# Transposing two weight matrices by DMA from DRAM instead of on TensorE, with the input loads on three queues

## The chip, the cores and the metric

The kernel runs on one core of one Trainium2 chip. The metric is device time in microseconds (us); lower is better. The engines are named as in the profile: PE (TensorE, matrix products; PEld is its weight load), DVE (VectorE), ACT (ScalarE), POOL (GpSimd), SP (SyncE). Every run quoted here as a time was marked fast (a run over 1.5% above the fastest of its kernel would be marked slow). Single profiled probes of one core are used for durations inside the trace, not for times. Each kernel was profiled once.

## The reference, cut to what matters

Two layers, each a linear attention followed by a gated MLP, over one sequence of 2048 rows and width 512, all in bf16:

```python
qkv = (x_norm @ wqkv).reshape(B, S, 3, H, Dh)            # H = 32 heads of Dh = 16
pk  = einsum("bhsd,hdf->bhsf", k, w_phi)                 # per head: k @ w_phi ; pq likewise
phi = concat([softmax(pk), softmax(-pk)])                # and the same for pq
kv, z = sum over s of phi_k^T v, sum over s of phi_k     # then num / den with phi_q, then @ wo
x = x + attention(layernorm(x));  x = x + mlp(layernorm(x))      # twice
```

The kernel multiplies `w_phi` into the weights once: `Wk2 = Wk @ Wblk` and `Wq2 = Wq @ Wblk`, where `Wblk` holds `w_phi` as diagonal blocks. This is called folding. The kernel writes that product as `matmul(..., lhsT=wT, rhs=Wblk)`, with Wk as `wT`: Wk with its *output* dimension on the partitions, that is, transposed. The whole change is about how that transposed copy is made, and when.

## The kernel before

Loads: SP's queue brings X, ScalarE's queue brings the weights. Wk and Wq come as they are.

```python
nc.gpsimd.dma_start(out=wf[:], in_=...w_phi...)
nc.sync.dma_start(out=st.X[0][:, 0:2, :], in_=xv[:, 0:2, :])
nc.scalar.dma_start(out=wk[:], in_=wv[:, :, D:2 * D])
nc.sync.dma_start(out=st.X[0][:, 2:4, :], in_=xv[:, 2:4, :])
nc.scalar.dma_start(out=wv_t[:], in_=wv[:, :, 2 * D:3 * D])
for c in range(1, st.NC):
    nc.sync.dma_start(out=st.X[c][:], in_=xv[:, c * TPC:(c + 1) * TPC, :])
nc.scalar.dma_start(out=wq[:], in_=wv[:, :, 0:D])
nc.scalar.dma_start(out=wo[:], in_=...)
```

Folding transposes on PE, copies on ACT, multiplies on PE, and copies on DVE:

```python
def fold(name, w):
    dst = const.tile([P, NDB, D], BF16, name=name)
    wT = st.big.tile([P, NDB, D], BF16, name="wT", tag="hT")
    for m in range(NDB):                                   # NDB = 4
        tps = st.ps_a.tile([P, NDB, P], BF16, name="tps", tag="a")
        for b in range(NDB):
            nc.tensor.transpose(out=tps[:, b, :], in_=w[:, m, b * P:(b + 1) * P], identity=ident[:])
        nc.scalar.copy(out=wT[:, :, m * P:(m + 1) * P], in_=tps[:])
    for m in range(NDB):
        wps = ...                                          # 4 matmuls wT x Wblk
        nc.vector.tensor_copy(out=dst[:, m, :]..., in_=wps[:])
    return dst
st.Wk2 = fold("Wk2", wk)
st.fold_q = lambda: fold("Wq2", wq)
```

Each tile of 128 rows is normalised on ACT (`xn`, from the row statistics and `nm`, the negated mean times the reciprocal deviation) and transposed by a DMA on SP's queue (`xnTA`). The key stage then makes per tile `kps` (keys), `vps` (values) and `kvq` (the sum over rows); `R` is built at its end. Wq is folded in one block before tile 10:

```python
def ahead(t):
    if t % 2 == 0 and t + 4 < st.T:
        with tc.issue_after(first.ins):
            A.norm(t + 4, 2)                # statistics, nm, xn and xnTA of two later tiles
    if 2 <= t < 9:
        st.load_B(A.moved)                  # two of the MLP's weight loads on SP's queue
    if t == 10:
        st.Wq2 = st.fold_q()
weave(A.keys(0, st.T, lag=2, pin=True, each=ahead), 1.0, none, 1.0)
```

The softmax here doesn't subtract the row's maximum and nothing guards it: scores larger than these inputs give would overflow.

## Time and profile before

| | before |
|---|---|
| median of 3 runs | 450.06 us (449.75 to 451.85) |
| span of the profiled execution | 446.8 us |
| first key matmul (`kps`) starts | 16.22 us |
| tile 9 / tile 10 of the keys start | 39.99 / 48.67 us |
| `R` starts, end of the key stage | 66.8 us |

These are lines of the page of the kernel before. In part 1, an engine's busy time is followed by its share and its instructions. In part 2 each position is a fortieth of the span (11.2 us). In part 6 the last number is the median time from issue to landing.

```profile
span 446.8 us, 7042 instructions
...
PE 394.1 (88%) x2508; PEld 226.2 (51%) x2508; DVE 276.4 (62%) x604; ACT 287.5 (64%) x653; POOL 70.1 (16%) x88
...
DMA  8659400211111121132001000011211132120010
GB/s 247 177 129 296 99 0 13 42 31 35 38 25 35 37 59 37 27 79 48 1 16 33 1 13 12 12 37 35 54 43 47 38 70 49 34 60 25 13 36 23
...
X<-in_A_x_dram SPq DMA_DIRECT2D x3, 512.0 KB, 11.5
```

PE is the limit over the whole span. Only the first slices are different: there the DMA engines are busy and PE waits. The table by stretch (start:end, length, busy time of each engine with its instructions, then granted clock, DMA share, GB/s) shows how full the DMA engines are at the start:

```profile
4.00:6.00 2.00, 0.03 (x1) 0.03 (x2) 1.21 (x3) 0.00 (x0) 0.00 (x0) 1.00 1.08 382
...
8.00:10.00 2.00, 0.59 (x6) 0.59 (x6) 1.38 (x9) 1.65 (x6) 0.00 (x0) 1.00 1.11 350
...
12.00:14.00 2.00, 0.41 (x4) 0.31 (x3) 2.00 (x5) 0.93 (x2) 0.00 (x0) 1.00 1.09 385
14.00:16.00 2.00, 0.17 (x2) 0.00 (x0) 2.00 (x7) 0.00 (x0) 0.00 (x0) 1.00 1.19 327
```

The chain of waits that ends last goes through the start like this (start, duration, what):

```profile
1.32 5.41 DMA X<-in_A_x_dram
...
8.79 0.58 ACT wT L109
...
10.58 5.59 DMA xnTA<-xn
...
16.22 1.04 PE kps L199 x2
```

The second loss is seen in the timeline of PE around the fold of Wq (start, duration, engine, line, operation; in brackets the idle time before it, and what ended that):

```profile
39.99 1.03 PE L199 MATMUL kps<-Wk,xnTA 128*128 128x512 bf16 x4
...
45.48 0.38 PE L108 MATMUL tps<-ident,wq 128*128 128x128 bf16 x4 [0.76 <-ACT wT L109]
...
48.44 0.40 PE L113 MATMUL wps<-Wblk,wT 128*128 128x128 bf16 x4 [1.49 <-ACT wT L109]
48.67 1.03 PE L199 MATMUL kps<-Wk,xnTA 128*128 128x512 bf16 x4
```

From tile 9 to tile 10 there are 8.7 us, where later tiles take 2.2. This is what the change aims at.

### The profile page before, as it was taken

How to read it: one execution, taken by the hardware profiler on the slowest of the kernel's cores; microseconds unless marked ns; L12 is line 12 of the kernel's file. 1: busy time of each engine (PE TensorE's matmuls, PEld its weight loads, DVE VectorE, ACT ScalarE, POOL GpSimd, SP SyncE). 2: the span in 40 equal slices, each digit the busy share in tenths (PEclk: the TensorE clock that was granted, in tenths of full speed). 3: DMA queues.
4: the chain of work that ended last, by engine and by line, in shares of the span. 5: the costliest groups of instructions: out<-in, count | busy, mean ns of one | idle time of the engine just before them, and what ended most of it. 6: DMA issues, size and time to landing. Idle time of an engine off the chain costs nothing.

```text
span 446.8 us, 7042 instructions
## 1 busy us (share of the span) xinstructions
PE 394.1 (88%) x2508; PEld 226.2 (51%) x2508; DVE 276.4 (62%) x604; ACT 287.5 (64%) x653; POOL 70.1 (16%) x88
## 2 busy tenths in 40 slices
PE   2688788899988999979998998778998899999996
PEld 2244444367756444435445744336675644444474
DVE  4795767737677777647465755773676676742232
ACT  4598756995846476599645749686584646736442
POOL 1077480000000000014323431000000000000000
PEclk9999999999999999999999999998999999999999
DMA  8659400211111121132001000011211132120010
GB/s 247 177 129 296 99 0 13 42 31 35 38 25 35 37 59 37 27 79 48 1 16 33 1 13 12 12 37 35 54 43 47 38 70 49 34 60 25 13 36 23
DMA packets 61458, 23.57 MB, mean 53 GB/s; under 512 B 52864, under 2 KB 60400, under 8 KB 61424
## 3 DMA queue, kind: packets, MB, share of 16 engines
q1 hardware_dynamic: 59280, 21.02, 20.6%
q10 hardware_dynamic: 2112, 2.10, 1.5%
q8 instruction: 19, 0.31, 0.3%
q14 instruction: 15, 0.12, 0.1%
q0 software_dynamic: 32, 0.02, 0.0%
HBM read 8.44 MB, written 2.10 MB: 24 GB/s over the span
## 4 chain that ended last, share of the span: by engine, by line
PE 57%; ACT 18%; DMA 9%; DVE 6%; issue 6%; POOL 2%; SPq 0%; POOLq 0%; ACTq 0%; DVEq 0%
PE ybps L394 13%; PE gps L377 12%; PE ups L384 12%; ACT xn L156 5%; PE yaps L314 4%; PE kps L199 4%; PE qps L268 4%; PE vps L209 4%; DMA oT<-o 3%; DMA xnTA<-xn 3%; PE kvq L238 2%; ACT junk L360 2%; ACT ru L387 2%; DMA xnTB<-xn 2%; ACT Eq L270 1%
## 5 line engine op out<-in xcount | busy, mean ns | idle before, releaser
L377 PE MATMUL gps<-xnTB,wg 128*128 128x256 bf16 (+3 forms) x528 | 99.7, 310 | 4.1 <-DMA xnTB<-xn 2.1
L384 PE MATMUL ups<-xnTB,wu 128*128 128x256 bf16 (+3 forms) x528 | 99.2, 310 | 3.3 <-ACT rg L380 3.3
L388 DVE TENSOR_TENSOR hT<-rg,ru 128x256 bf16<-128x256 bf16 (+3 forms) x132 | 48.7, 370 | 64.3 <-ACT ru L387 63.8
L394 PE MATMUL ybps<-wd,hT 128*128 128x512 bf16 (+1 forms) x352 | 80.8, 379 | 2.7 <-ACT ru L387 2.0
L380 ACT ACTIVATE rg<-gps 128x256 bf16<-128x256 f32 (+3 forms) x132 | 60.0, 454 | 34.2 <-PE gps L377 31.8
L221 POOL TENSOR_TENSOR phiK<-ek,sk 128x1024 bf16<-128x1024 bf16 x30 | 57.8, 1929 | 88.2 <-DVE sk L218 38.6
L387 ACT CAST ru<-ups 128x256 bf16<-128x256 f32 (+3 forms) x132 | 58.1, 440 | 18.1 <-PE ups L384 13.8
L377 PEld LDWEIGHTS <-wg 128*128 128x128 bf16 (+1 forms) x528 | 52.3, 101 | 32.8 <-DMA xnTB<-xn 3.4
L384 PEld LDWEIGHTS <-wu 128*128 128x128 bf16 (+1 forms) x528 | 52.6, 101 | 29.3 <-issue 4.3
L216 DVE TENSOR_REDUCE sk<-ek 128x64 f32<-128x1024 bf16 x32 | 38.9, 1217 | 31.1 <-ACT ek L205 30.9
L394 PEld LDWEIGHTS <-hT 128*128 128x128 bf16 (+1 forms) x352 | 34.3, 98 | 43.9 <-issue 2.8
L156 ACT ACTIVATE xn<-X,nm,rstd 128x512 bf16<-128x512 bf16 x64 | 49.7, 813 | 9.1 <-DMA xnTA<-xn 5.5
L360 ACT ACTIVATE junk<-X,mean 128x512 bf16<-128x512 bf16 x32 | 23.1, 721 | 36.8 <-POOL mean L357 36.5
L292 DVE TENSOR_TENSOR Tn<-erq,rS 128x816 bf16<-128x816 f32 x64 | 45.9, 717 | 1.0
L397 DVE TENSOR_TENSOR X<-X,ybps 128x512 bf16<-128x512 bf16 x32 | 21.9, 685 | 30.8 <-PE ybps L394 30.5
L357 POOL TENSOR_SCALAR mean<-xsum 128x1 f32<-128x1 f32 x32 | 7.1, 223 | 208.8 <-DVE X L320 104.8
L199 PE MATMUL kps<-Wk,xnTA 128*128 128x512 bf16 x128 | 34.2, 389 | 5.2 <-DMA xnTA<-xn 4.8
L268 PE MATMUL qps<-xnTA,Wq 128*128 128x512 bf16 x128 | 32.5, 378 | 6.8 <-ACT Eq L271 6.2
L314 PE MATMUL yaps<-wo,oT 128*128 128x512 bf16 x128 | 33.7, 379 | 4.0 <-DMA oT<-o 4.0
L209 PE MATMUL vps<-wv,xnTA 128*128 128x512 bf16 x128 | 33.9, 387 | 0.0
L291 DVE RECIPROCAL rS<-erq 128x48 f32<-128x48 f32 x64 | 22.4, 350 | 15.5 <-PE erq L282 15.5
L204 ACT ACTIVATE ek<-kps 128x512 bf16<-128x512 f32 x32 | 19.1, 596 | 13.9 <-PE kps L199 13.9
(58 smaller groups left out, 388.7 us busy)
## 6 DMA issues: line engine op xcount, KB each, us to landing
out_dram<-X SPq DMA_DIRECT2D x16, 128.0 KB, 1.7
X<-in_A_x_dram SPq DMA_DIRECT2D x3, 512.0 KB, 11.5
wg<-in_B_W_gate_dram SPq DMA_DIRECT2D x4, 344.0 KB, 4.7
wu<-in_B_W_up_dram SPq DMA_DIRECT2D x4, 344.0 KB, 5.8
wd<-in_B_W_down_dram SPq DMA_DIRECT2D x5, 256.0 KB, 4.4
wk<-in_A_wqkv_dram ACTq DMA_DIRECT2D x1, 512.0 KB, 5.1
X<-in_A_x_dram SPq DMA_DIRECT2D x2, 256.0 KB, 4.7
wv<-in_A_wqkv_dram ACTq DMA_DIRECT2D x1, 512.0 KB, 8.0
```

The lines of the kernel that those rows point to most:

```text
L156: nc.scalar.activation(out=xn[:], in_=st.X[c][:, t0 + i, :], func=AF.Identity, scale=rstd[:, i:i + 1], bias=nm[:, i:i + 1])
L199: mm = nc.tensor.matmul(kps[:], lhsT=xnT[:, b, ts], rhs=st.Wk2[:, b, :], start=(b == 0), stop=(b == NDB - 1))
L209: mm = nc.tensor.matmul(vps[:], lhsT=xnT[:, b, ts], rhs=st.wv[:, b, :], start=(b == 0), stop=(b == NDB - 1))
L221: eng.tensor_tensor(out=phiK[:].rearrange("p s (h f) -> p (s h) f", f=DH), in0=ek[:].rearrange("p s (h f) -> p (s h) f", f=DH), in1=sk[:]. ...
L268: nc.tensor.matmul(qps[:], lhsT=st.Wq2[:, m, b * P:(b + 1) * P], rhs=self.xnT[c][:, m, :], start=(m == 0), stop=(m == NDB - 1))
L314: nc.tensor.matmul(yps[:], lhsT=oT[:, b, :], rhs=st.wo[:, b, :], start=(b == 0 and not on_pe), stop=(b == NDB - 1))
L377: nc.tensor.matmul(gps[:n, 0:w], lhsT=st.wg[:, b, f * P:f * P + n], rhs=xnT[:, b, 0:w], start=(b == 0), stop=(b == NDB - 1))
L380: nc.scalar.activation(out=rg[:n, 0:w], in_=gps[:n, 0:w], func=AF.Relu)
L384: nc.tensor.matmul(ups[:n, 0:w], lhsT=st.wu[:, b, f * P:f * P + n], rhs=xnT[:, b, 0:w], start=(b == 0), stop=(b == NDB - 1))
L387: nc.scalar.copy(out=ru[:n, 0:w], in_=ups[:n, 0:w])
L388: nc.vector.tensor_tensor(out=hT[:n, f, 0:w], in0=rg[:n, 0:w], in1=ru[:n, 0:w], op=Alu.mult)
L394: nc.tensor.matmul(yps[:], lhsT=hT[:n, f, (t - lo) * P:(t - lo + 1) * P], rhs=st.wd[:n, f, :], start=(f == 0), stop=(f == NFT - 1))
```

## The change

The intent: let the DMA engines transpose Wk and Wq on their way from DRAM (I call each such transfer of 128 rows, 128 KB, a *flip*), so that PE's 32 transposes and ACT's 8 copies go away; spread the input loads over three queues so that they are issued sooner; and spread the fold of Wq over tiles 6 to 9 so that no tile waits for all of it. Line numbers in the profiles are those of each kernel's own file.

```diff
+    def flip(dst, off):
+        for m in range(NDB):
+            st.moved = nc.sync.dma_start_transpose(out=dst[:, :, m * P:(m + 1) * P],
+                                                   in_=A_wqkv[m * P:(m + 1) * P, off:off + D])
     nc.gpsimd.dma_start(out=wf[:], ...)
-    nc.sync.dma_start(out=st.X[0][:, 0:2, :], in_=xv[:, 0:2, :])
-    nc.scalar.dma_start(out=wk[:], in_=wv[:, :, D:2 * D])
-    nc.sync.dma_start(out=st.X[0][:, 2:4, :], in_=xv[:, 2:4, :])
+    nc.scalar.dma_start(out=st.X[0][:, 0:2, :], in_=xv[:, 0:2, :])
+    flip(wkT, D)
+    nc.scalar.dma_start(out=st.X[0][:, 2:4, :], in_=xv[:, 2:4, :])
     nc.scalar.dma_start(out=wv_t[:], in_=wv[:, :, 2 * D:3 * D])
-    for c in range(1, st.NC):
-        nc.sync.dma_start(out=st.X[c][:], ...)
-    nc.scalar.dma_start(out=wq[:], in_=wv[:, :, 0:D])
-    nc.scalar.dma_start(out=wo[:], ...)
+    nc.scalar.dma_start(out=st.X[1][:], in_=xv[:, TPC:2 * TPC, :])
+    st.flip_q = lambda: flip(wqT, 0)
 ...  (masks for Wblk on GpSimd)
+    for c in range(2, st.NC):
+        nc.gpsimd.dma_start(out=st.X[c][:], ...)
+    nc.gpsimd.dma_start(out=wo[:], ...)
 ...
-    def fold(name, w):  (transposes on PE, copies on ACT, four products)
+    def fold(dst, wT, m):  (one of the four products; copy on DVE for even m, on ACT for odd m)
+    for m in range(NDB):
+        fold(st.Wk2, wkT, m)
+    st.fold_q = lambda m: fold(st.Wq2, wqT, m)
 ...
+        if t == 0:
+            st.flip_q()
-        if 2 <= t < 9:
+        if 3 <= t < 10:
             st.load_B(A.moved)
-        if t == 10:
-            st.Wq2 = st.fold_q()
+    def also(t):
+        if 6 <= t < 10:
+            st.fold_q(t - 6)
```

The diff also adds an `on_pool` branch to the normalisation, which is never taken, and cuts the query stage into one function per block (not shown; the order of its instructions stays).

More of the change, by code (lines that the diff above doesn't have):

```diff
@@ L56, in setup @@
     st.X = [const.tile([P, TPC, D], BF16, name=f"X{c}") for c in range(st.NC)]
-    wk = st.big.tile([P, NDB, D], BF16, name="wk", tag="Eq", bufs=4)
+    wkT = st.big.tile([P, NDB, D], BF16, name="wkT", tag="Eq", bufs=4)
+    wqT = st.big.tile([P, NDB, D], BF16, name="wqT", tag="Eq", bufs=4)
     wv_t = const.tile([P, NDB, D], BF16, name="wv")
-    wq = st.big.tile([P, NDB, D], BF16, name="wq", tag="Eq", bufs=4)
     wf = const.tile([P, NDB, DH], BF16, name="wf")
     wo = const.tile([P, NDB, D], BF16, name="wo")
+    def flip(dst, off):
+        for m in range(NDB):
+            st.moved = nc.sync.dma_start_transpose(out=dst[:, :, m * P:(m + 1) * P],
+                                                   in_=A_wqkv[m * P:(m + 1) * P, off:off + D])
     nc.gpsimd.dma_start(out=wf[:], in_=A_w_phi.rearrange("(b j) d f -> (j d) b f", b=NDB, j=8))
-    nc.sync.dma_start(out=st.X[0][:, 0:2, :], in_=xv[:, 0:2, :])
-    nc.scalar.dma_start(out=wk[:], in_=wv[:, :, D:2 * D])
-    nc.sync.dma_start(out=st.X[0][:, 2:4, :], in_=xv[:, 2:4, :])
+    nc.scalar.dma_start(out=st.X[0][:, 0:2, :], in_=xv[:, 0:2, :])
+    flip(wkT, D)
+    nc.scalar.dma_start(out=st.X[0][:, 2:4, :], in_=xv[:, 2:4, :])
     nc.scalar.dma_start(out=wv_t[:], in_=wv[:, :, 2 * D:3 * D])
     nc.scalar.preload_act_table_set("natural_log_exp_and_others")
-    for c in range(1, st.NC):
-        nc.sync.dma_start(out=st.X[c][:], in_=xv[:, c * TPC:(c + 1) * TPC, :])
-    nc.scalar.dma_start(out=wq[:], in_=wv[:, :, 0:D])
-    nc.scalar.dma_start(out=wo[:], in_=A_wo.rearrange("(b p) f -> p b f", p=P))
+    nc.scalar.dma_start(out=st.X[1][:], in_=xv[:, TPC:2 * TPC, :])
     st.wv, st.wo = wv_t, wo
+    st.flip_q = lambda: flip(wqT, 0)
     st.eps = const.tile([P, 1], F32, name="eps")
@@ L85, in setup @@
     st.M8f = M8f
+    for c in range(2, st.NC):
+        nc.gpsimd.dma_start(out=st.X[c][:], in_=xv[:, c * TPC:(c + 1) * TPC, :])
+    nc.gpsimd.dma_start(out=wo[:], in_=A_wo.rearrange("(b p) f -> p b f", p=P))
     M8 = const.tile([P, 8], BF16, name="M8")
@@ L100, in setup, with fold @@
         st.vext.append(v)
-    def fold(name, w):
-        dst = const.tile([P, NDB, D], BF16, name=name)
-        wT = st.big.tile([P, NDB, D], BF16, name="wT", tag="hT")
-        for m in range(NDB):
-            tps = st.ps_a.tile([P, NDB, P], BF16, name="tps", tag="a")
-            for b in range(NDB):
-                nc.tensor.transpose(out=tps[:, b, :], in_=w[:, m, b * P:(b + 1) * P], identity=ident[:])
-            nc.scalar.copy(out=wT[:, :, m * P:(m + 1) * P], in_=tps[:])
-        for m in range(NDB):
-            wps = st.ps_b.tile([P, NDB, P], F32, name="wps", tag="b")
-            for b in range(NDB):
-                nc.tensor.matmul(wps[:, b, :], lhsT=wT[:, b, m * P:(m + 1) * P], rhs=Wblk[:, b, :],
-                                 start=True, stop=True)
-            nc.vector.tensor_copy(out=dst[:, m, :].rearrange("p (b f) -> p b f", f=P), in_=wps[:])
-        return dst
-    st.Wk2 = fold("Wk2", wk)
-    st.fold_q = lambda: fold("Wq2", wq)
+    st.Wk2 = const.tile([P, NDB, D], BF16, name="Wk2")
+    st.Wq2 = const.tile([P, NDB, D], BF16, name="Wq2")
+    def fold(dst, wT, m):
+        wps = st.ps_b.tile([P, NDB, P], F32, name="wps", tag="b")
+        for b in range(NDB):
+            nc.tensor.matmul(wps[:, b, :], lhsT=wT[:, b, m * P:(m + 1) * P], rhs=Wblk[:, b, :],
+                             start=True, stop=True)
+        out_ = dst[:, m, :].rearrange("p (b f) -> p b f", f=P)
+        if m % 2:
+            nc.scalar.copy(out=out_, in_=wps[:])
+        else:
+            nc.vector.tensor_copy(out=out_, in_=wps[:])
+    for m in range(NDB):
+        fold(st.Wk2, wkT, m)
+    st.fold_q = lambda m: fold(st.Wq2, wqT, m)
     st.wg = const.tile([P, NDB, F], BF16, name="wg")
@@ L137, in setup, with apply_norm @@
     return st
-def apply_norm(st, c, t0, n, var, scale, mean, sign, dst, col):
+def apply_norm(st, c, t0, n, var, scale, mean, sign, dst, col, on_pool=False):
     nc = st.nc
@@ L155, in apply_norm, with norm_tiles @@
         xn = st.work.tile([P, D], BF16, name="xn")
-        nc.scalar.activation(out=xn[:], in_=st.X[c][:, t0 + i, :], func=AF.Identity,
-                             scale=rstd[:, i:i + 1], bias=nm[:, i:i + 1])
+        if on_pool:
+            nc.gpsimd.tensor_scalar(out=xn[:], in0=st.X[c][:, t0 + i, :], scalar1=rstd[:, i:i + 1],
+                                    scalar2=nm[:, i:i + 1], op0=Alu.mult, op1=Alu.add)
+        else:
+            nc.scalar.activation(out=xn[:], in_=st.X[c][:, t0 + i, :], func=AF.Identity,
+                                 scale=rstd[:, i:i + 1], bias=nm[:, i:i + 1])
         moved = nc.sync.dma_start_transpose(out=dst[:, :, (col + i) * P:(col + i + 1) * P], in_=xn[:])
     return last, moved
-def norm_tiles(st, c, t0, n, dst, col):
+def norm_tiles(st, c, t0, n, dst, col, on_pool=False):
     nc = st.nc
@@ L168, in norm_tiles @@
         nc.vector.bn_aggr(out=mv[:, i, :], in_=stats[:])
-    return apply_norm(st, c, t0, n, mv[:, 0:n, 1], 1.0, mv[:, 0:n, 0], -1, dst, col)
+    return apply_norm(st, c, t0, n, mv[:, 0:n, 1], 1.0, mv[:, 0:n, 0], -1, dst, col, on_pool)
 class LayerA:
@@ L178, in __init__, with norm, keys @@
         self.moved = None
-    def norm(self, t, n=1):
+    def norm(self, t, n=1, on_pool=False):
         c, ti = t // TPC, t % TPC
-        last, self.moved = norm_tiles(self.st, c, ti, n, self.xnT[c], ti)
+        last, self.moved = norm_tiles(self.st, c, ti, n, self.xnT[c], ti, on_pool)
         return last
-    def keys(self, lo, hi, on_dve=(), lag=1, pin=False, each=None):
+    def keys(self, lo, hi, on_dve=(), lag=1, pin=False, each=None, also=None):
         st, nc = self.st, self.st.nc
@@ L229, in keys @@
                 yield 2.3
+            if also is not None:
+                also(t)
         for k in late:
@@ L260, in build_R, with query, queries @@
                                            op0=Alu.add, op1=Alu.mult)
-    def queries(self, c):
+    def query(self, c, b, keep=lambda ins: ins):
         st, nc = self.st, self.st.nc
-        self.Eq[c] = Eq = st.big.tile([P, NDB, 2, CH], BF16, name="Eq", bufs=st.NC)
-        for b in range(NDB):
-            qps = st.ps_a.tile([P, CH], F32, name="qps", tag="a")
-            for m in range(NDB):
-                nc.tensor.matmul(qps[:], lhsT=st.Wq2[:, m, b * P:(b + 1) * P], rhs=self.xnT[c][:, m, :],
-                                 start=(m == 0), stop=(m == NDB - 1))
-            nc.scalar.activation(out=Eq[:, b, 0, :], in_=qps[:], func=AF.Exp, scale=1.0)
-            nc.scalar.activation(out=Eq[:, b, 1, :], in_=qps[:], func=AF.Exp, scale=-1.0)
+        if b == 0:
+            self.Eq[c] = st.big.tile([P, NDB, 2, CH], BF16, name="Eq", bufs=st.NC)
+        Eq = self.Eq[c]
+        qps = st.ps_a.tile([P, CH], F32, name="qps", tag="a")
+        for m in range(NDB):
+            mm = nc.tensor.matmul(qps[:], lhsT=st.Wq2[:, m, b * P:(b + 1) * P], rhs=self.xnT[c][:, m, :],
+                                  start=(m == 0), stop=(m == NDB - 1))
+            if m == 0:
+                keep(mm)
+        nc.scalar.activation(out=Eq[:, b, 0, :], in_=qps[:], func=AF.Exp, scale=1.0)
+        nc.scalar.activation(out=Eq[:, b, 1, :], in_=qps[:], func=AF.Exp, scale=-1.0)
+    def queries(self, c, lo=0):
+        for b in range(lo, NDB):
+            self.query(c, b)
             yield 4
@@ L453, in ahead @@
                 A.norm(t + 4, 2)
-        if 2 <= t < 9:
+        if t == 0:
+            st.flip_q()
+        if 3 <= t < 10:
             st.load_B(A.moved)
-        if t == 10:
-            st.Wq2 = st.fold_q()
-    weave(A.keys(0, st.T, lag=2, pin=True, each=ahead), 1.0, none, 1.0)
-    weave(A.queries(0), QC, none, 1.0)
+    def also(t):
+        if 6 <= t < 10:
+            st.fold_q(t - 6)
+    weave(A.keys(0, st.T, lag=2, pin=True, each=ahead, also=also), 1.0, none, 1.0)
+    weave(A.queries(0), 1.0, none, 1.0)
     qs = seq(*[A.queries(c) for c in range(1, NC)]), 3 * QC
```

## The prediction

> **What bounds the kernel now.** Over the whole span TensorE is the limit (part 1 of the page: PE 394.1 of 446.8 us, 88%). The change touches only what lies before 67 us, where PE is not full: windows give PE busy 3.9 of the first 16.0 us, 23.5 of 16–42, 3.3 of 42–49, 13.0 of 49–62. After that the instruction order of both kernels is the same, so the key stage's gain should pass through one to one.
>
> Two losses are in reach:
> 1. The start. DMA moves about 350 GB/s from 4 to 16 us. The first row transpose (xnTA) issues at 10.58 and lands at 16.2, behind the X loads on its own ring; the first key matmul (kps) starts at 16.22.
> 2. Folding Wq in one block. kps of tile 9 starts at 39.99, of tile 10 at 48.67: 8.7 us against 2.20 in tiles 10–15. PE waits for the wT copies (0.59 us each on ACT, queued behind normalisations), not for xnTA, which were there. About 6.5 us lost.
>
> **Removed.** 32 PE transposes (3 us), 8 ACT copies (4.7 us).
>
> **Added.** 8 transposes from DRAM on SP's queue. SP issues an SBUF transpose in 1.19 us, so 8 take about 9.6 us and the first xnTA can issue at about 10.5 us: as before. In DMA time a transpose costs about 0.64 us (two in 16–20 us, share 0.32), against 0.36 us for 128 KB at 350 GB/s: some 2 us more DMA. [...]I expect no more bandwidth in the first 16 us (two queues reach 350 GB/s here). xnTA 0 now stands behind the flips rather than the X loads: landing at 13–16.5 us.
>
> **Moved.** In the new order VectorE builds Wblk only after statistics and nm of the second X block (before: ahead of them, done at 9.1 us). That nm waits for rstd on ScalarE, which stands behind the fourth xn, which needs a buffer freed by xnTA 0. So: X1 about 12 us, xnTA 0 about 13–16.5, nm 15–17.5, Wblk 16–18.5, 16 fold matmuls, two bnst (1.3 us) ahead of two copies of Wk2 on VectorE (0.69 each); on ScalarE two copies behind two xn. First kps at 18.5–22.5 us, say 20.3: about 4 us LATER than before.
> Against it: eight xn instead of four are done before the first kps. ScalarE from there through tile 9 needs about 24 us (1.48 per tile, 0.78 per xn, small ones, two Wq copies), PE 22.8 (1.73 + 0.47 per tile, 4 x 0.43 fold). So tile 10 starts 24.5–25.5 us after the first kps (before 32.4), at about 45.4 instead of 48.67. The on_pool branch is never taken.
>
> **Net.** -6.5 (block of Wq) +1.7 (fold spread) -2 (fewer ACT stalls) +4 (later start): about -3.2 us, all on the critical path. I predict 446.8 us, 442.5 to 451.5 (8 in 10); faster by over 2% 0.10, within 2% 0.85, slower 0.05.
>
> **What would show it.** Timeline: first kps at 18.5–22.5 us, PE waiting on Wblk (VectorE), not on wkT; no gap over 3.5 us between key tiles 5 and 11; last kvq near 63.5 us (before 66.75); everything after 67 us merely shifted; DMA near 350 GB/s until about 16 us.
>
> **What would make it wrong.** Transposes from DRAM issuing or moving much slower than those from SBUF (xnTA 0 late, loss at the start over 7 us); [...]X1 landing late behind wv; or Wblk earlier than the order suggests (gain 6–7 us).

[...] stands for the ground given for expecting no more bandwidth in the first 16 us, which so stands as an assumption, and for one of the cases under "What would make it wrong". The sum came to about -3.2 us as the author put it, from -6.5, +1.7, -2 and +4 (which add up to -2.8).

## The result, and the profile after

| | before | after |
|---|---|---|
| median of the fast runs | 449.96 us (449.75 to 451.85) | 467.3 us (464.43 to 467.87) |
| ratio of the fast runs, 95% interval | | 1.0363 (1.032 to 1.0406) |
| span of the profiled execution | 446.8 us | 462.7 us |
| first `kps` | 16.2 us | 29.7 us |
| from first `kps` to `R` | 50.6 us | 47.9 us |
| from `R` to the end | 380.0 us | 385.1 us |

A ratio here is the mean time of one kernel's fast runs over the mean of the other's of the same rounds, so it is not quite the ratio of the medians beside it. The changed kernel is slower by 3.6%, where 446.8 us was predicted. In the profiled executions the 15.9 us split as follows, in differences of the table's last three rows: +13.5 at the start, -2.7 in the key stage, +5.1 afterwards.

The page of the kernel after, the lines that answer to those above, and the head of its part 4 (shares of the span in the chain that ended last):

```profile
span 462.7 us, 6982 instructions
...
PE 391.0 (85%) x2476; PEld 223.6 (48%) x2476; DVE 277.4 (60%) x600; ACT 286.5 (62%) x649; POOL 72.3 (16%) x91
...
DMA  8954920121012012223101100012111222221010
GB/s 170 178 107 97 306 56 0 24 53 29 20 40 47 12 35 45 47 41 62 35 1 24 23 1 20 6 23 58 35 45 35 57 55 50 28 57 42 12 35 23
...
PE 54%; ACT 17%; DVE 8%; DMA 7%; issue 5%; SPq 5%; POOL 2%; POOLq 0%; ACTq 0%; DVEq 0%
...
X<-in_A_x_dram POOLq DMA_DIRECT2D x2, 512.0 KB, 14.4
```

PE lost 3 us of work, as intended. But SPq, the queue that issues DMAs on SP, is now 5% of the chain; its share was 0% before. The same table by stretch:

```profile
4.00:6.00 2.00, 0.00 (x0) 0.00 (x0) 2.00 (x6) 0.58 (x3) 1.37 (x3) 1.00 0.98 157
...
8.00:10.00 2.00, 0.00 (x0) 0.00 (x0) 0.16 (x1) 1.22 (x3) 0.00 (x0) 1.00 1.00 230
...
12.00:14.00 2.00, 0.00 (x0) 0.00 (x0) 0.00 (x0) 0.00 (x0) 0.00 (x0) 1.00 0.97 179
14.00:16.00 2.00, 0.00 (x0) 0.00 (x0) 0.00 (x0) 0.00 (x0) 0.00 (x0) 1.00 1.12 144
```

The DMA share is near 1 in both kernels. What it moves in that time has halved: 385 GB/s became 179. A share near 1 does not tell here how fast the engines move data. The chain of waits at the start, after:

```profile
0.81 1.30 SPq L65
...
9.93 9.12 SPq L65
...
22.51 2.55 DMA xnTA<-xn
...
25.10 2.43 DMA xnTA<-xn
...
27.56 0.81 ACT xn L166
```

The eight flips are issued one after the other from 0.81 to 22.4 us. One of them holds SP's queue for 9.12 us. The first row transpose stands behind them in that queue and is issued at 22.51 instead of 10.58 us. The timeline of the start, after:

```profile
0.81 7.32 SPq L65 DMA_TRANSPOSE wkT<-in_A_wqkv_dram  x4
...
8.17 14.22 SPq L65 DMA_TRANSPOSE wqT<-in_A_wqkv_dram  x4
...
22.58 1.29 DVE L177 BATCH_NORM_STATS2 bnst<-X 128x6 f32<-128x512 bf16 x2 [13.98 <-DMA X<-in_A_x_dram]
...
26.67 0.66 DVE L96 TENSOR_TENSOR Wblk<-M,wf 128x512 bf16<-128x512 bf16 x1
...
27.38 1.44 PE L115 MATMUL wps<-Wblk,wkT 128*128 128x128 bf16 x12 [27.38 <-DVE Wblk L96]
...
29.70 1.70 PE L209 MATMUL kps<-Wk,xnTA 128*128 128x512 bf16 x4
```

Two things come late and end together. DVE waits 13.98 us for the second X block, which is on ScalarE's queue behind Wv. `Wblk`, which needs nothing but the small `w_phi`, stands behind that block's work on DVE, so the fold of Wk starts only at 27.38 us.

The trace keeps a record of every DMA packet with its ring (one per issuing engine; in the kernel after 19.97 MB went over SP's, 1.57 over ScalarE's and 1.59 over GpSimd's), size, start and duration. Adding up the KB by ring for each microsecond of the kernel after gives this (first two columns: plain loads; a flip or row transpose moves packets of 256 bytes):

| us | GpSimd's loads, packets of 4096 B | ScalarE's loads, 1024 B | SP's transposes, 256 B |
|---|---|---|---|
| 3 | none yet | 207 | 125 |
| 8 | 140 | 72 | 25 |
| 11 | 132 | 13 | 22 |
| 12 | 128 | 26 | 12 |
| 13 | 132 | 36 | 16 |
| 14 | 76 | 64 | 17 |
| 15 | 60 | 52 | 13 |
| 22 | done | done | 211 |
| 23 | done | done | 254 |

Alone, the transposes (from 22.5 us on, row transposes among them) move 211 to 254 KB per us. Beside the two other rings, from 5 to 21 us, they move 10 to 62, mostly under 30. The packets themselves are slower too: those of 4096 B last 169 ns in the median, but 345 ns in the mean and up to 3121 ns (in a2_plain below, without flips, 166, 174 and at most 302); those of 256 B 18 ns in the median, 32 in the mean and up to 916.

After the key stage the two kernels have the same instruction order. Matching ACT's and DVE's instructions of the same group one by one gives the shift of the kernel after, in the time of the kernel before: +10.8 us from 65 to 85 us, +11.4 at 120, then three steps, to +14.7 at 137, +15.5 at 159 and +17.0 at 197, and back to +15.2 by 310. So the shift of the key stage was not passed on one to one.

### The profile page after: what moved, and what is told of

It is laid out like the page before. It is cut to its first block, busy times and chain, and to the rows that moved or that the text cites. A ratio compares the mean times of both kernels' runs of the same rounds, so it can differ in the third digit from the quotient of the medians.

```text
span 462.7 us, 6982 instructions
## 1 busy us (share of the span) xinstructions
PE 391.0 (85%) x2476; PEld 223.6 (48%) x2476; DVE 277.4 (60%) x600; ACT 286.5 (62%) x649; POOL 72.3 (16%) x91
## 3 DMA queue, kind: packets, MB, share of 16 engines
q1 hardware_dynamic: 61504, 19.97, 20.6%
q0 software_dynamic: 464, 1.59, 1.9%
q10 hardware_dynamic: 1600, 1.57, 1.4%
## 4 chain that ended last, share of the span: by engine, by line
PE 54%; ACT 17%; DVE 8%; DMA 7%; issue 5%; SPq 5%; POOL 2%; POOLq 0%; ACTq 0%; DVEq 0%
PE ybps L413 13%; PE gps L396 12%; PE ups L403 11%; ACT xn L166 5%; SPq L65 5%; PE yaps L333 4%; DMA oT<-o 4%; PE vps L219 4%; PE kps L209 3%; PE qps L281 3%; DMA xnTA<-xn 3%; PE kvq L250 2%; DVE sk L226 2%; ACT junk L379 2%; ACT ru L406 2%
## 5 line engine op out<-in xcount | busy, mean ns | idle before, releaser
L406 ACT CAST ru<-ups 128x256 bf16<-128x256 f32 (+3 forms) x132 | 58.1, 440 | 21.6 <-PE ups L403 17.1
L403 PEld LDWEIGHTS <-wu 128*128 128x128 bf16 (+1 forms) x528 | 52.6, 101 | 29.7 <-issue 5.2
L166 ACT ACTIVATE xn<-X,nm,rstd 128x512 bf16<-128x512 bf16 x64 | 49.9, 812 | 23.9 <-DMA xnTA<-xn 19.6
L310 DVE RECIPROCAL rS<-erq 128x48 f32<-128x48 f32 x64 | 22.4, 350 | 15.8 <-PE erq L301 15.8
L177 DVE BATCH_NORM_STATS2 bnst<-X 128x6 f32<-128x512 bf16 x32 | 21.2, 674 | 16.4 <-DMA X<-in_A_x_dram 16.1
```

The source lines that it names most:

```text
L166: nc.scalar.activation(out=xn[:], in_=st.X[c][:, t0 + i, :], func=AF.Identity, scale=rstd[:, i:i + 1], bias=nm[:, i:i + 1])
L403: nc.tensor.matmul(ups[:n, 0:w], lhsT=st.wu[:, b, f * P:f * P + n], rhs=xnT[:, b, 0:w], start=(b == 0), stop=(b == NDB - 1))
L406: nc.scalar.copy(out=ru[:n, 0:w], in_=ups[:n, 0:w])
```

## The experiments

Twelve kernels ran, in three calls on three chips; each call timed its own runs of the kernel before. All twelve gave outputs that the comparison with the reference accepted. The theories, in words (where a recorded expectation numbers its theories, those numbers are its own; number 5 is the instruction-fetch theory):

- **Crawl:** in the company of other rings' loads the flips get a small part of the bytes, and the DMA engines together move less.
- Rivals to it: **slow source** (a transpose from DRAM is slow by itself); **queues** (moving plain loads to other queues makes the loss, whatever the flips are).
- **Order:** `Wblk` stands behind the second X block on DVE.
- **Block:** the 6.5 us of the fold of Wq in one block are lost to the fold. Rival, **backlog:** they are mostly ScalarE's backlog of work that is paid anyway.
- **Instruction fetch** (theory 5): with fewer PE instructions, PE's fetches of instructions fall at other moments and collide with urgent transposes. Rival, **clock dips**.

### a1_spread: the kernel before, with the fold of Wq spread

```diff
+    def fold_q_T(m): (four PE transposes of wq, ACT copy)     +    def fold_q_W(m): (four products, DVE copy)
-        if t == 10:
-            st.Wq2 = st.fold_q()
+    def also(t):
+        if 7 <= t < 11:
+            st.fold_q_T(t - 7)
+        if 8 <= t < 12:
+            st.fold_q_W(t - 8)
```

> The kernel before with one part of the change alone: Wq is folded over four key tiles (its PE transposes and ACT copies kept, spread over tiles 7 to 10, the products over 8 to 11). If the block at 42-49 us cost about 6.5 us as the prediction said, the gap of 8.7 us before key tile 10 falls to about 3 us and the time falls by 3.5 to 5.5 us, to 444.5-446.5 us. Rival: ScalarE, not the block, sets the pace there, and the eight extra steps only move: gain under 1.5 us.

Measured: 449.34 us against 450.0, ratio 0.9983 (0.9945 to 1.002). The interval of the times includes no change and leaves out the 3.5 us that were expected at least. `R` starts at 65.3 us, 1.5 us earlier than in the kernel before. The timeline of PE at the same place:

```profile
39.39 1.02 PE L216 MATMUL kps<-Wk,xnTA 128*128 128x512 bf16 x3 [1.20 <-ACT ek L222]
...
42.04 1.03 PE L216 MATMUL kps<-Wk,xnTA 128*128 128x512 bf16 x4
...
45.49 0.81 PE L216 MATMUL kps<-Wk,xnTA 128*128 128x512 bf16 x3 [0.38 <-ACT ek L222]
```

The hole of 8.7 us is gone, but now tile 7 takes 4.5 us and tiles 8 to 11 2.5 to 3.5 us each, waiting for ACT (`ek`), and the end of the stage moves by 1.5 us only. Backlog is right: the block was a place where ACT caught up, so filling it saved 1.5 us of the key stage and not 3.5 to 5.5.

### a2_plain: the kernel after, with plain loads in place of the flips

The weights then stand untransposed in `wkT` and `wqT`, so this kernel computes something else. (The comparison accepted it all the same; it is not sensitive to this, and the verdict "correct" of this run says nothing.)

```diff
-            st.moved = nc.sync.dma_start_transpose(out=dst[:, :, m * P:(m + 1) * P],
-                                                   in_=A_wqkv[m * P:(m + 1) * P, off:off + D])
+            nc.sync.dma_start(out=dst[:, m, :], in_=A_wqkv[m * P:(m + 1) * P, off:off + D])
```

> The kernel after, with the eight transposes from DRAM replaced by eight plain loads of the same 128 KB on the same queue (wrong result on purpose, the weights stay untransposed). Three queues, the order of the engines and the spread stay. Theory 1 (transposes of 256-byte packets lose against, and stall with, the loads of other rings): loads now end at about 14-17 us, SP issues the eight in about 5 us, first kps at 19-21 us, time 448-452 us. Theory 3 (loads issued by GpSimd slow all traffic): loads still end after 20 us, first kps after 26 us, time over 460 us.

Measured: 460.05 us, ratio 1.0228 (1.0193 to 1.0264); both theories had forecast something else (448 to 452 us, or over 460 with the first `kps` after 26 us). First `kps` at 23.2 us, `R` at 72.6. Two stretches of the table that was shown before:

```profile
8.00:10.00 2.00, 0.00 (x0) 0.00 (x0) 0.16 (x1) 1.59 (x3) 0.00 (x0) 1.00 1.06 373
...
12.00:14.00 2.00, 0.00 (x0) 0.00 (x0) 0.00 (x0) 0.00 (x0) 0.00 (x0) 1.00 1.04 381
```

Three rings of plain loads keep the rate of two: 353 to 381 GB/s from 8 to 14 us, where two moved 349 to 385 in the kernel before. The third queue brings no more bandwidth here, and loses none either. But they share it unevenly. From 8 to 12 us the rings get 200 to 248 KB per us (GpSimd, 4096 B), 56 to 73 (ScalarE, 1024 B) and 56 to 73 (SP, 1024 B): about 4 to 1 to 1, as the packet sizes. What makes these shares is not shown. The second X block, on ScalarE's ring, is late here even without flips: its statistics start at 17.51 us, in the kernel before at 11.0. The timeline of a2_plain has it beside ACT's wait for the first row transpose:

```profile
17.51 1.29 DVE L176 BATCH_NORM_STATS2 bnst<-X 128x6 f32<-128x512 bf16 x2 [8.55 <-DMA X<-in_A_x_dram]
17.75 0.81 ACT L165 ACTIVATE xn<-X,nm,rstd 128x512 bf16<-128x512 bf16 x1 [7.94 <-DMA xnTA<-xn]
```

That row transpose was issued at 8.00 us and landed at 17.73, just after the last plain weight load of its own queue (17.23). `Wblk` follows at 20.45.

Of the 13.5 us at the start this kernel keeps 7.0 (23.2 - 16.2); those come from the queues and the order, the eight loads ahead of the row transposes on SP's queue included. The other 6.5 go when the flips stop being transposes. So neither the crawl nor the queues alone is the answer.

### a3_nopool: the kernel after, without loads on GpSimd's queue

```diff
+    st.flip_q()                              # all eight flips first
     for c in range(2, st.NC):
-        nc.gpsimd.dma_start(out=st.X[c][:], ...)
-    nc.gpsimd.dma_start(out=wo[:], ...)
+        nc.sync.dma_start(out=st.X[c][:], ...)
+    nc.sync.dma_start(out=wo[:], ...)
```

> The kernel after, with X2, X3 and wo issued by SP behind the eight transposes and nothing large on the GpSimd queue, so that the transposes share the engines with the scalar queue's ring of 1024-byte packets alone. Theory 1 with the GpSimd ring's 4096-byte packets as the main cause: transposes move 100 KB per us, SP has issued all eight by about 12 us, first kps at 19-23 us, time 447-454 us. Theory 2 (a transpose from DRAM is slow by itself): the eight still take over 20 us, first kps after 29 us, time over 464 us. In between (first kps at 24-28 us): any other ring hurts, not only GpSimd's.

Measured: 458.44 us, ratio 1.0182 (1.0143 to 1.0222). The eight flips are issued in 1.3 us each, from 0.8 to 11.3 us, close to what the prediction had (1.19 us each). First `kps` at 20.2 us, inside the predicted 18.5 to 22.5; `R` at 68.7, only 1.9 us later than before; tile 10 starts 29.0 us after the first `kps`. The rest of its loss, up to +7.9, comes later, with three clock dips after the key stage where the kernel before had one, and with the steps of instruction fetches that e_pad below deals with. So without the loads on GpSimd's ring the flips are issued at full speed, beside ScalarE's ring alone. The edit also moves those loads behind the flips in time, so it does not tell whether their ring, their packet size or a third stream as such did the harm. The total is still low, 218 to 228 GB/s from 4 to 10 us. The time missed its forecast of 447 to 454 us.

### a4_lateq: the kernel after, with the flips of Wq late

```diff
-        if t == 0:
-            st.flip_q()
+        if t == 6:
+            with tc.issue_after(A.moved.ins):
+                st.flip_q()
-        if 6 <= t < 10:
-            st.fold_q(t - 6)
+        if 10 <= t < 14:
+            st.fold_q(t - 10)
```

> The kernel after, with the four transposes of Wq issued after the row transposes of key tile 11 and folded at tiles 10 to 13: half of the transposes leave the crowded start and nothing stands between wkT and the first row transpose on SP. Theory 1: wkT is still starved beside the loads (lands at 12-18 us), first row transpose issues at 9-12 us, first kps at 19-24 us, time 449-457 us. Theory 2 (DRAM transposes slow by themselves, some 2.5 us each): wkT lands by 11 us, and the late wqT takes 10 us in a quiet stretch, too, which the fold then waits for.

Measured: 463.61 us, ratio 1.0314 (1.027 to 1.0358), where 449 to 457 us was expected. With four flips fewer in front of it, the first row transpose is issued at 8.3 us and yet the first `kps` starts at 23.5, about as in a2_plain: `Wblk` (20.7 us) holds it. The late flips are quick, issued in 1.3 to 1.7 us each. But they stand in SP's queue ahead of row transposes and MLP weights, and now ACT waits for a buffer that a row transpose has to free. Its timeline:

```profile
56.33 0.81 ACT L166 ACTIVATE xn<-X,nm,rstd 128x512 bf16<-128x512 bf16 x1 [4.61 <-DMA xnTA<-xn]
```

Three tiles of the keys then take 4.3 to 4.5 us each instead of 2.2, and `R` starts at 74.9. Fewer flips at the start bring the first `kps` 6.2 us forward against the kernel after, and 3.5 of these are given back by the end of the key stage (77.6 against 74.9).

### p_alone, p_act, p_pool: the disputed cost by itself

Each is the kernel before with four extra flips of Wq that nobody reads, at key tile 11 or 12, in a quiet moment: alone, beside 1.4 MB of loads on ScalarE's queue (1024-byte packets), or beside the same 1.4 MB on GpSimd's queue (4096-byte packets). p_alone also has four transposes from SBUF.

```diff
+        for m in range(NDB):
+            src = wv_t[:, m, :] if kind == "sbuf" else A_wqkv[m * P:(m + 1) * P, 0:D]
+            nc.sync.dma_start_transpose(out=s[:, :, m * P:(m + 1) * P], in_=src)
+            (p_act, p_pool: before these, three loads of wo of 512, 512 and 384 KB on the other queue)
```

> A measuring kernel: the kernel before, with four extra transposes of Wq from DRAM into an unused tile in the quiet stretch after key tile 11, and four transposes of the same size from on-chip memory after key tile 14. Theory 1 (transposes are slow only in company): both sources issue at 1.2-1.3 us each, both move four in about 5 us (up to 250 KB per us), 256-byte packets at a median of 18-20 ns in both, landing 2.4-4 us after issue. Theory 2 (DRAM as a source is slow by itself): the DRAM ones take at least twice as long per packet or to landing (over 6 us).

> A measuring kernel: the kernel before, with four transposes of Wq from DRAM into an unused tile after key tile 12, beside 1.4 MB of plain loads that ScalarE's queue issues at the same moment (1024-byte packets). Theory 1 ([...]a ring's share goes with its packet size): while both run, the transposes get about a fifth of the bytes, some 60-80 KB per us against 260-300, and the first lands 4-6 us after issue. Rival (rings share bytes evenly): about half each, and 128 KB lands in about 2.5 us.

> A measuring kernel: the same with the 1.4 MB issued by GpSimd (4096-byte packets). Theory 1: while both run, the transposes get about a seventeenth of the bytes, some 10-25 KB per us against 200-350, and the first lands over 5 us after issue. Rival (rings share bytes evenly): about half each. If the sum falls below 300 KB per us while both run, company costs throughput besides the share.

The DMA issues of p_alone, with the median time from issue to landing last; then of p_act; then of p_pool:

```profile
probe_dram<-in_A_wqkv_dram SPq DMA_TRANSPOSE x4, 2.8
probe_sbuf<-wv SPq DMA_TRANSPOSE x4, 2.5
```

```profile
side_act<-in_A_wo_dram ACTq DMA_DIRECT2D x2, 512.0 KB, 6.2
...
probe_act<-in_A_wqkv_dram SPq DMA_TRANSPOSE x4, 7.0
```

```profile
side_pool<-in_A_wo_dram POOLq DMA_DIRECT2D x2, 512.0 KB, 5.6
...
probe_pool<-in_A_wqkv_dram SPq DMA_TRANSPOSE x4, 6.1
```

Slow source falls: alone, a flip from DRAM is issued in 1.26 us and lands in 2.8, against 1.27 and 2.5 from SBUF. In company the same flips need 5.7 to 8.5 us (ScalarE's loads) or 2.7 to 7.9 us (GpSimd's) to land. Their issue stays quick, 1.2 to 1.4 us each. So company slows the landing, but company alone does not hold SP's queue: with four flips nothing was held. Where it was held for over 5 us, in the kernel after (9.12 us), e_pad (8.38), b_order (7.51) and a4_lateq (5.13), it was each time the sixth transpose of SP's queue, in a4_lateq a row transpose. In a3_nopool the sixth was not held, and no run shows what held the others. Per byte a transpose's packet is the slower kind even alone: 256 bytes took 18 ns (p_alone, and in the median the kernel before), 1024 bytes of a plain load 46 to 52 (the kernel before), which is 1.4 to 1.6 times as long per byte. The KB per us in the packet records of the two, flips / loads:

| us | p_act | p_pool |
|---|---|---|
| 58 | 75 / 7 | 123 / 0 |
| 59 | 48 / 63 | 5 / 52 |
| 60 | 1 / 331 | 0 / 312 |
| 61 | 0 / 295 | 122 / 148 |
| 62 | 5 / 328 | 130 / 60 |
| 63 | 106 / 108 | 2 / 76 |
| 64 | 45 / 163 | 6 / 28 |
| 65 | 104 / 113 | 4 / 292 |

I had expected a fixed share by packet size. That is not what happens. The two kinds come in bursts: the flips stand still for up to three microseconds while the loads run at 295 to 331 KB per us, then both run together at a sum of 213 to 222 GB/s (p_act, 63 to 65 us), or both nearly stop (p_pool, 35 GB/s at 64 us, with single 4096-byte packets of up to 1982 ns). What in the DMA engines makes this is not visible in a trace, and I leave it open. What is shown is its effect: in company the median landing of a transpose more than doubles (7.0 and 6.1 us against 2.8), and the total falls.

### e_pad: the kernel after, with PE's number of instructions restored

```diff
+    for m in range(8):                       # 32 dead transposes at PE's start, while it waits anyway
+        tps = st.ps_a.tile([P, NDB, P], BF16, name="tps", tag="a")
+        for b in range(NDB):
+            nc.tensor.transpose(out=tps[:, b, :], in_=ident[:], identity=ident[:])
```

> The kernel after, with 32 dead PE transposes at the head, where PE waits anyway, so that PE's instruction stream is as long as before's again. After the key stage the kernel after loses 3-5 us more, in steps, at the same places in all kernels derived from it, whatever the shift of the key stage. Theory 5 (PE's instructions are fetched by DMA, 16 KB at a time; 64 instructions fewer move the fetches to moments at which a row transpose on the same engine is urgent): the steps at 135-160 us of before's time vanish, the time falls by 1.5-3 us against the kernel after, to about 464-465.5 us. Rival (the later loss comes from the shift of the key stage, or from the granted clock alone): the steps stay.

Measured: 462.26 us (457.59 to 463.57), ratio 1.0297 (1.0241 to 1.0352), where 464 to 465.5 us was expected. In its profiled execution, the fastest of its four runs, the shift is +7.7 us at the end of the key stage and +8.3 at 369 us; in the kernel after the same stretch went from +10.8 to +15.2. The steps at 137, 159 and 197 us are gone. (The mean granted clock of this execution is 0.969, since it was halved from 10.8 to 31.3 us, while PE mostly waited for the start.)

The place where the first step arises, in the timeline of PE, first before and then after:

```profile
137.27 1.04 PE L314 MATMUL yaps<-wo,oT 128*128 128x512 bf16 x4 [1.70 <-DMA oT<-o]
```

```profile
150.37 1.77 PE L333 MATMUL yaps<-wo,oT 128*128 128x512 bf16 x4 [3.37 <-DMA oT<-o]
```

PE waits 3.37 us for a transpose of the attention output where it waited 1.70. That transpose landed 4.1 us after its issue, against 2.4 in the kernel before and in e_pad. The queue of instruction fetches (19 packets, 0.31 MB: 16 KB each) shows a fetch at 148.2 us of 921 ns, just while that transpose was under way; in the kernel before the nearest fetch came at 130.7 us, and in e_pad at 139.0, which is again 130.7 in the time of the kernel before. At the step at 159 it is the same: a fetch at 170.8 us in the kernel after, while a transpose of the same kind took 3.3 us to land instead of 2.4 in e_pad. PE has 64 instructions fewer (the matmuls and weight loads of part 1 of the page: 2508 each became 2476 each), and the sixth fetch comes after 1459 of them in the kernel before and 1454 in the kernel after, so the fetches fall elsewhere in the program. From one fetch to the next PE starts 254 of them in the mean in the kernel before (228 to 286) and 256 in the kernel after (230 to 288), by the start times in the traces; this is why I take the queue to be PE's. Each of these two fetches coincided with a transpose that landed late, by 1.7 and 0.9 us; how the one delays the other is not shown.

One pair of kernels would be thin evidence. Over all runs it reads like this: the step at 137 us is there in all seven profiled kernels that have fewer PE instructions than the kernel before (after, a2_plain, a3_nopool, a4_lateq, b_order, v1_mix, v2_defer; 0.7 to 1.7 us where no clock dip fell in) and in none of the six that have as many (a1_spread, e_pad, v2_pad and the three probes).

The rest of the steps are dips: for 3.4 us the granted clock of PE halves, which costs about 1.5 us. The profiled execution before had one (at 303 us) and the one after two (150.5 and 208.6). Seven of the kernels have a step at 197 us with a dip in that place (a1_spread, a2_plain, a3_nopool, a4_lateq, b_order and p_act besides the kernel after), and e_pad, without a dip there, has no step. So of the 4.4 us that the kernel after lost between 65 and 369 us, about 2.4 are the two steps of instruction fetches (1.6 at 137 us, taken from a2_plain where no dip was, and 0.8 at 159); 0.6 is a small step at 91 us that e_pad has too and that stays unexplained; the rest is dips. The spread of e_pad's own runs, 6 us, is too wide to confirm this by times; it rests on the profiled executions.

### b_order: the kernel after, with `Wblk` first

```diff
+    with tc.issue_after(last.ins):           # last: the second mask operation on GpSimd
         for c in range(2, st.NC):
             nc.gpsimd.dma_start(out=st.X[c][:], ...)
 ...
-            with tc.issue_after(first.ins):
+            with tc.issue_after(first.ins), tc.issue_after(st.wblk.ins):
                 A.norm(t + 4, 2)
```

> The kernel after, with GpSimd's loads issued behind its three mask instructions, which lets VectorE build Wblk right after the first statistics, as before, and not behind those of X1. Only the order of instructions differs. The prediction said that this order delays the first kps. If so: Wblk done by 10 us, first kps at 25.5-27.5 us (kernel after: 29.7, with the fold of Wk done before xnTA 0 lands at 25.1), time 463-465.5 us. Rival: transposes and X1 set the first kps, the order costs nothing: first kps at 29 us or later.

Measured: 460.33 us, ratio 1.0251 (1.0213 to 1.0288), where 463 to 465.5 us was expected. From the timeline of its start:

```profile
7.63 0.69 DVE L97 TENSOR_TENSOR Wblk<-M,wf 128x512 bf16<-128x512 bf16 x1
...
17.31 0.61 PE L116 MATMUL wps<-Wblk,wkT 128*128 128x128 bf16 x4 [6.80 <-DMA wkT<-in_A_wqkv_dram]
...
22.55 0.61 PE L210 MATMUL kps<-Wk,xnTA 128*128 128x512 bf16 x1
```

`Wblk` is done at 8.3 us, and now the fold waits for the flips themselves (6.80 us). The first row transpose is issued at 19.9 us here, as in e_pad (19.8), whose `kps` starts at 27.4, and `kps` starts as soon as it has landed. Against that one the order is worth 3.5 to 4.9 us of the first `kps` (the first matmul at 22.6, the next at 23.9), by one profile of each. `R` starts at 73.3 against 74.5, so most of it is given back by the end of the key stage. Order is right as a mechanism and small as a cost.

### v1_mix: the kernel before, with Wq flipped late and its fold spread

This is the version that the experiments point to: leave the crowded start alone, take from the change only what falls in a quiet moment.

```diff
-    nc.scalar.dma_start(out=wq[:], in_=wv[:, :, 0:D])
+    def flip_q(m):
+        nc.sync.dma_start_transpose(out=wqT[:, :, m * P:(m + 1) * P], in_=A_wqkv[m * P:(m + 1) * P, 0:D])
+    def fold_q(m): (four products, copy on DVE)
 ...
+        if t in (0, 2):
+            with tc.issue_after(A.moved.ins):
+                st.flip_q(t)
+                st.flip_q(t + 1)
-        if t == 10:
-            st.Wq2 = st.fold_q()
+    def also(t):
+        if 6 <= t < 10:
+            st.fold_q(t - 6)
```

> A version meant to beat both: the kernel before, without its load of Wq and its PE transposes and ACT copies of Wq; four DMA transposes of Wq are issued in gaps of SP's queue after the start's loads are through (two after the row transpose of key tile 5, two after that of tile 7), and the fold is spread over tiles 6 to 9 with all copies on VectorE. Theory 1: the transposes move 128 KB in about 1 us there, as nothing else moves; the key stage gains the 2.4 us of ScalarE copies on top of the 1.5 us of the spread alone: end of the key stage 3-4.5 us earlier than before, time 446-448 us unless the instruction fetches move badly (32 PE instructions fewer; up to +3 us). Rival (transposes of Wq by DMA cost wherever they stand): no gain, 450 us or more.

Measured: 447.38 us (445.69 to 449.26, six runs), ratio 0.9953 (0.9926 to 0.998). The flips are issued from 22.4 to 31 us, in 1.3 to 2.1 us each. First `kps` at 14.9 us, 1.3 earlier than before, with 512 KB less to load ahead of the first row transposes; `R` at 64.3, 2.5 earlier. It beats both kernels: by about 2 us the one before (0.5%, clear of no change but within the 2% that the record calls "same"), and the one after by some 20 (of another call). The step of the instruction fetch at 137 us takes back 1.1 us of it.

### v2_defer and v2_pad: more room at the start, and the fetch once more

v2_defer is v1_mix with the last X block loaded after the fourth row transpose and `wo` loaded with the MLP's weights. v2_pad is v2_defer with 16 dead PE transposes in front, so that PE has as many instructions as in the kernel before.

```diff
-    for c in range(1, st.NC):
+    for c in range(1, st.NC - 1):
         nc.sync.dma_start(out=st.X[c][:], ...)
+    with tc.issue_after(A.moved.ins):        # after the first four row transposes
+        st.late_loads()                      # the last X block
+    (v2_pad only:) for m in range(4): four nc.tensor.transpose of the identity
```

> The version above, with X3 and wo deferred: X3 is loaded after the row transpose of tile 3, wo with the MLP's weights. The start then loads 2.5 MB instead of 4 MB, and the first row transpose no longer waits behind X3. Expected: the first kps at 14-15.5 us instead of 16.2, end of the key stage 4-6 us earlier than before, time 444.5-447 us (again up to +3 us if instruction fetches move badly). Rival: the fold of Wk sets the first kps (done at 15.3 us before): then 16 us and no gain over the version above.

> The version above (v2_defer) with 16 dead PE transposes at the head of PE, where it waits for the first load, so that PE's instruction stream has the length that it has before. Theory 5 (position of the instruction fetches): after the key stage its times run parallel to those of before (no steps of over 1 us other than dips of the clock), so it is faster than v2_defer by what that one loses in steps, 0 to 3 us: 443.5-446 us. Rival: no difference, or a loss from the extra PE work (about 1.5 us of PE time while it waits).

Measured: v2_defer 448.18 us, ratio 0.9973 (0.9949 to 0.9996); v2_pad 449.02 us, ratio 0.9978 (0.9956 to 1.0). In v2_defer the row transposes are early (the first issued at 9.0 us), but the first `kps` starts at 16.0 us, as the rival had it: PE waited 6.37 us for ACT's copies of the transposed Wk. More room for the transposes brings nothing once the fold of Wk is last. v2_pad runs parallel to the kernel before after the key stage (shift -0.4 at 65 us, -0.6 at 369), where v2_defer loses about 1 us of its lead (-2.3 to -1.2), 0.7 of it at 137 us: in the traces the fetch theory holds a second time. In the times it brought nothing: v2_pad is no faster than v2_defer and missed its 443.5 to 446 us, since the dead transposes cost its start 1.5 us. Padding is no way to gain.

## Why the prediction was wrong

Point by point, as the prediction put it:

- **"8 take about 9.6 us and the first xnTA can issue at about 10.5 us."** This is the step that failed first. They took 21.6 us, one alone 9.12, and the first xnTA was issued at 22.51. The cost of a transpose was read in the kernel before, where no transpose runs beside another ring's loads, and was used for a place where three rings are full. a3_nopool shows the premise (1.3 us each) right without GpSimd's loads in flight, and p_alone shows it for flips alone.
- **"In DMA time a transpose costs about 0.64 us ... some 2 us more DMA."** Right alone (211 to 254 KB per us from 22.5 us on, so 128 KB in 0.5 to 0.6 us); in company the total falls to 144 to 230 GB/s (stretches from 4 to 22 us), where the kernel before had 306 to 385 (4 to 16 us). "DMA near 350 GB/s until about 16 us" failed with it. That the total would hold with flips among the loads was the author's assumption: the start of the kernel before, from which the 350 GB/s were read, has plain loads alone.
- **"X1 about 12 us."** 22.6. The change moved the block to a ring that gets a small part of the bytes (56 to 73 KB per us of ScalarE's beside 200 to 248 of GpSimd's in a2_plain). a2_plain, with 17.5 us against 11.0 in the kernel before, shows that 6.5 us of this come without any flip.
- **"Wblk 16-18.5"** and the first `kps` at 18.5 to 22.5 us, behind `Wblk` and not behind `wkT`: the mechanism was right, the times 27.3 and 29.7 us were not, since X1 and the first row transpose were late. With `Wblk` early (b_order) 3.5 to 4.8 us of the first `kps` go.
- **"-6.5 (block of Wq)."** Mis-sized: with the +1.7 for the spread it makes 4.8 us, and a1_spread, which spreads and does nothing else, gained 1.5. The hole on PE was taken for a cost of the fold, where ACT's backlog stood behind it. The key stage as a whole gained 2.7 us instead of the 7.2 that a net of -3.2 with a later start of +4 implies (the prediction's own four terms add up to -2.8 and not -3.2); tile 10 was to start 24.5 to 25.5 us after the first `kps`, and started 29.1 us after it. One more delay shows in the trace of the kernel after: three `nm` operations on DVE, of 128x2 elements, took 3.65 us together while GpSimd ran `phiK`:

```profile
38.08 3.81 POOL L231 TENSOR_TENSOR phiK<-ek,sk 128x1024 bf16<-128x1024 bf16 x2 [0.72 <-DVE sk L228]
38.27 3.65 DVE L156 SCALAR_TENSOR_TENSOR nm<-mv,rstd 128x2 f32<-128x2 f32 x3
```

  In the kernel before one takes 0.10 to 0.45 us; here the longest lasted 1.89 us, and each `phiK` 1.92 to 1.93. No run took this delay away, so neither its cause nor its part in the time is shown.
- **"The key stage's gain should pass through one to one"; "everything after 67 us merely shifted."** Failed by 5.1 us in the profiled executions: two collisions of instruction fetches with urgent transposes (about 2.4 us), one clock dip more, and some tenths that stay unexplained. The order of instructions was the same; the DMAs that fetch them were not counted as part of it.
- **What would make it wrong.** The prediction named small transposes losing against plain loads (the passage that is cut from it), and "X1 landing late behind wv". Both happened (mostly under 30 KB per us for the flips from 5 to 21 us, and 22.58 us for the statistics of X1 against 11.0), though not as a fixed share by packet size (p_act, p_pool). It gave all of "slower" 5%. The loss of the start was known to be possible, but its size was not worked out.

What stays open: why the total rate falls when transposes and plain loads are in flight together, why single packets then last up to 3 us, and why SP's queue was held for 9.12 us by the sixth transpose and not by others. The split of the start, 6.5 us for the flips and 7.0 for queues and order, rests on one profile of each kernel.

## What to carry to other kernels

A DMA transpose that was cheap in a quiet moment (2.8 us from issue to landing in p_alone) was not cheap beside other queues' loads (7.0 and 6.1 us in p_act and p_pool, and eight issued in 21.6 us at the start): put it where the queues are idle, as v1_mix does, and keep the first urgent transfer of a queue ahead of it (in a4_lateq, with the first row transposes ahead of Wq's flips, the first `kps` came 6.2 us earlier than in the kernel after). When loads are spread over queues, ask which ring gets the bytes (in a2_plain the ring of 4096-byte packets got four times those of the others), and judge DMA by GB/s and by landing times rather than by its busy share (near 1 at 385 GB/s and at 179). A hole on the limiting engine can be worth only what the next engine's backlog leaves of it (1.5 us of 6.5 in a1_spread): spread the work once in the old kernel, and measure, before counting the hole as gain.
